# Loading the first keys by heads on two queues, and a finer list of operations, in a gated delta rule with a softplus block on one core

## The chip, the core and the metric

The program runs on one core of a Trainium2 chip. A core has five engines that run their own instruction streams in order and meet at semaphores: TensorE (PE, matmuls; PEld is its weight load), VectorE (DVE), ScalarE (ACT), GpSimd (POOL) and SyncE (SP). Transfers between device memory (HBM) and the on-chip memory (SBUF) run on 16 DMA engines and are issued by SP, ACT or POOL. Matmul results land in PSUM, here eight banks.

The metric is the device time of one execution in microseconds (us). A profile is one execution taken by the hardware profiler; its span goes from the first to the last instruction.

## The reference

Inputs are q, k, v and g of shape (4 batches, 8 heads, 768 steps, 48 features), beta of (4, 8, 768), and two weights: w_in (384, 2048) and w_out (2048, 384). All are float32.

```python
k_n = k / (np.linalg.norm(k, axis=-1, keepdims=True) + 1e-06)
state = zeros(B, H, D, D)
for t in range(S):
    readout = einsum('bhd,bhde->bhe', q[:, :, t], state)
    y[:, :, t] = g[:, :, t] * readout
    v_old = einsum('bhde,bhd->bhe', state, k_n[:, :, t])
    state = state + beta[:, :, t] * einsum('bhd,bhe->bhde', k_n[:, :, t], v[:, :, t] - v_old)
x = y.transpose(0, 2, 1, 3).reshape(B * S, H * D)
h = x @ w_in
out = (maximum(h, 0) + log1p(exp(-abs(h)))) @ w_out
```

The first part is a recurrence over 768 steps in 32 independent pairs of batch and head; the second is a dense block, two matmuls with a softplus between them.

## The kernel before

**Chunks.** The 768 steps are cut into 12 chunks of 64. Inside a chunk the recurrence becomes matrix algebra: the Gram matrix of the chunk's keys, a triangular system whose inverse is needed, and products with the state that the chunk before left. Two batches lie on the two halves of the 128 partitions (e = 0 and 1), two more side by side (p = 0 and 1), and each tile holds eight heads.

**The front of a chunk** (functions `norms` and `front`): the keys are squared (`ksq`, line 402) and summed per head (`red`, line 413), a square root and 1e-6 give the norms (`sqrt`, `eps`). The raw keys of chunks 0 and 1 are cast to 16 bits (`cast`; later chunks are scaled first, `kmul`), transposed by PE (`trs`, line 526), evicted from PSUM (`kev`), and the Gram matmuls follow (`gramk` for keys by keys, `gramq` for keys by queries, line 598). The key Gram is evicted with its sign turned (`kkc`, tile kk), the query Gram is masked (`mask`, tile mt). Chunks 0 and 1 do this in two halves of four heads.

**The inverse** (`inverse`) works on groups of chunks: 0, then 1, then pairs (2, 3), (4, 5) up to (10, 11); a group is named after its first chunk. The Gram is brought into lanes by 32 by 32 transposes on DVE (`ln`, line 656), picked (`pick`), and multiplied by beta (`prep`, line 697). `lbeta` prepares beta for the unscaled keys of chunks 0 and 1; it needs the selection matmuls `bsel` (line 287), which move beta from the partition of a head to lanes. Then come 15 steps j = 0 to 14 of a forward substitution: step 0 is one operation (line 709), every other a product into tmp (line 717) and an addition into tt (line 724), 29 operations in one serial string. They stand on DVE or POOL. `ca`, `cb` and `st` put the result back into matrix form (lines 738 and 779), and three rounds of PE matmuls (`xmm`, `tmm`, `zmm`) with evictions between them give the inverse of the whole chunk.

**The chain** (`chain`) is what carries the state from chunk to chunk: `ks` (state by keys, line 914), `w` (line 953), `umm`, `u1`, `zu`, `u2`, then `smm` and `s` (the new state, line 1010) and `qs`, `ymm` and `y` (the output times g, line 1036). `ytr` or a DMA transpose turns y into the columns of the dense block (tile xt).

**The dense block** (`dense`): `g1` multiplies by w_in into tile h (line 1088), `soft` is the softplus on ACT (line 1100), `g2` multiplies by w_out (line 1115), `o` evicts to tile osb, and `store` writes 64 rows at a time (line 1139).

**Order.** Nothing is scheduled by the hardware beyond the engines' own queues. Every piece of work is an item with a list of engines that may run it. The text `_ORDER` at the end of the file names each item once with its engine (D DVE, A ACT, G POOL, P PE, S SP); `Program.emit` walks through it and issues the items' instructions, so that the order on each engine is the order in that text. Tiles are taken from rings when an item first uses them and go back after the last use. An item that holds several instructions issues them together. Before the list the kernel issues a fixed head: the first beta load on ACT (line 184), the constants, and the identity.

Loads are items of SP (`load`, lines 326, 337 and 345). In this version chunk 0's keys are two loads, one for each half of the partitions:

```python
nc.scalar.dma_start(out=beta_n[:, : C * N_RAW], in_=beta_bt[:, : C * N_RAW])
```

```python
ENG[en].dma_start(
    out=b.ap[64 * e : 64 * e + 64].rearrange("t p h d -> t (p h) d"),
    in_=x[lo : lo + 2, :, ts].rearrange("p h t d -> t (p h) d"),
)
```

The list also holds filler matmuls (`fill`, line 1149), whose results nobody reads; of 96 that exist, `_ORDER` names 15.

## Time and profile before

| what | value |
|---|---|
| median of 3 timed runs | 295.17 us |
| the three runs | 381.88, 295.17, 240.01 us |
| the profiled execution | 239.09 us |
| its span, first to last instruction | 237.3 us |
| mean granted TensorE clock over the span | 0.984 |
| instructions | 11021 |
| HBM read and written | 25.26 and 4.72 MB |

The largest groups of instructions by busy time:

| group | instructions | busy us |
|---|---|---|
| g1, PE line 1088 | 384 | 74.0 |
| g2, PE line 1115 into tile o | 352 | 66.1 |
| softplus, ACT line 1100 | 96 | 56.5 |
| step products, POOL line 717 | 78 | 29.6 |
| step additions, POOL line 724 | 78 | 29.0 |
| powers for the norms, POOL line 427 | 8 | 23.5 |
| masks, DVE line 580 | 48 | 18.6 |

Rows of a timeline give the start in us from the beginning of the span, the length in us, the engine, the line, the operation, output and input tiles (buffer numbers left out), and in brackets how long the engine was idle before and what ended that. Consecutive instructions on one engine overlap slightly in these rows, since a row ends when the result is confirmed. A name such as SPq or ACTq is an engine's queue issuing a transfer. "issue" is time in which the engine waited for nothing that the profile shows. The chain of waits is followed back from the last instruction, step by step, to whatever released it.

### The profile page before, as it was taken

What the parts mean: (1) busy time and instruction counts of PE and PEld (TensorE: products, weight loads), DVE (VectorE), ACT (ScalarE), POOL (GpSimd) and SP (SyncE); (2) the same over time, 40 slices, a digit from 0 to 9 for tenths busy, and PEclk for the clock granted to TensorE, in tenths of its full rate; (3) what the DMA queues carried; (4) which work ended last, traced back from release to release, by engine and by line L of the source; (5) the groups of instructions that cost most, each with busy time, mean ns of one, the idle gap of its engine ahead of it and who ended that gap; (6) DMA issues with size and microseconds to landing.
All of it is one profiled execution on the core that took longest, in us unless ns stands there. A gap on an engine that the chain in (4) does not pass through costs nothing.

```text
span 237.3 us, 11021 instructions
## 1 busy us (share of the span) xinstructions
PE 206.0 (87%) x4787; PEld 130.4 (55%) x4787; DVE 162.8 (69%) x371; ACT 155.8 (66%) x332; POOL 115.3 (49%) x223
## 2 busy tenths in 40 slices
PE   4837865977987999989599999889999999999992
PEld 3723543754665665556355556455555555667761
DVE  7898994989978899995689768966648043521000
ACT  4999893955886789957189886348663766035520
POOL 5248989576767888988864763104721000000000
PEclk9999995999999999999999999999999999999999
DMA  6999999999899188789399676888635301242222
GB/s 117 179 196 171 194 205 210 185 146 188 151 181 149 37 150 153 204 134 151 86 162 154 119 143 77 130 174 155 116 89 115 69 7 33 64 92 50 53 50 66
DMA packets 101136, 30.30 MB, mean 128 GB/s; under 512 B 91808, under 2 KB 101056, under 8 KB 101088
## 3 DMA queue, kind: packets, MB, share of 16 engines
q1 hardware_dynamic: 96128, 24.96, 61.6%
q0 software_dynamic: 3712, 3.15, 9.3%
q10 hardware_dynamic: 1248, 1.49, 2.6%
q8 instruction: 37, 0.61, 1.1%
q14 instruction: 11, 0.09, 0.2%
HBM read 25.26 MB, written 4.72 MB: 126 GB/s over the span
## 4 chain that ended last, share of the span: by engine, by line
PE 63%; DVE 9%; issue 6%; ACT 6%; POOL 6%; DMA 5%; SPq 3%; DVEq 0%; ACTq 0%; POOLq 0%
PE h L1088 22%; PE o L1115 20%; PE d L598 3%; PE d L914 3%; PE d L1115 2%; SPq L345 2%; POOL tt L724 2%; DMA kqt<-kn 2%; POOL tmp L717 2%; PE d L1022 2%; DMA f<-in_k_dram 2%; ACT kk L222 2%; DMA f<-in_g_dram 2%; PE d L980 1%; DVE mt L580 1%
## 5 line engine op out<-in xcount | busy, mean ns | idle before, releaser
L1088 PE MATMUL h<-xt,w_in 128*128 128x512 f16 (+1 forms) x384 | 74.0, 330 | 0.3 <-DVE xt L224 0.2
L1100 ACT ACTIVATE ga<-h 128x512 f16<-128x512 f32 x96 | 56.5, 601 | 26.1 <-PE h L1088 21.2
L1115 PE MATMUL o<-w_out,ga 128*128 128x384 f16 x352 | 66.1, 327 | 0.0
L1115 PEld LDWEIGHTS <-ga 128*128 128x128 f16 x384 | 35.1, 98 | 22.3
L1088 PEld LDWEIGHTS <-w_in 128*128 128x128 f16 x384 | 35.1, 99 | 20.9 <-issue 0.7
L717 POOL TENSOR_TENSOR tmp<-nn,tt 128x56 f32<-128x56 f32 (+13 forms) x78 | 29.6, 379 | 19.9 <-DVE tt L724 12.1
L724 POOL TENSOR_TENSOR tt<-tt,tmp 128x56 f32<-128x56 f32 (+13 forms) x78 | 29.0, 372 | 6.1
L222 ACT ACTIVATE osb<-o 128x384 f32<-128x384 f32 x17 | 8.4, 492 | 25.1 <-PE o L1115 20.8
L427 POOL TENSOR_TENSOR nv<-nv,half_c 128x16 f32<-128x16 f32 x8 | 23.5, 2937 | 2.0 <-DVE nv L413 1.8
L580 DVE TENSOR_TENSOR mt<-d,mask 128x256 f16<-128x256 f32 x48 | 18.6, 410 | 4.8 <-ACT kk L222 2.2
L598 PE MATMUL d<-kqt 48*64 48x128 f16 (+1 forms) x448 | 11.4, 228 | 8.1 <-ACT kqt L222 4.6
L224 DVE CAST u<-d 128x384 f16<-128x384 f32 x21 | 11.4, 552 | 10.1 <-PE d L967 5.5
L1036 DVE TENSOR_TENSOR yg<-d,f 128x384 f16<-128x384 f32 x24 | 12.5, 546 | 8.4 <-ACT ga L1100 4.5
L222 ACT ACTIVATE u<-d 128x384 f16<-128x384 f32 x27 | 12.8, 494 | 6.0 <-PE d L980 3.2
L598 PEld LDWEIGHTS <-kqt 48*64 48x64 f16 x448 | 8.1, 118 | 14.8 <-issue 8.6
L222 ACT ACTIVATE kqt<-d 128x512 f16<-128x512 f16 (+1 forms) x23 | 14.1, 636 | 1.8 <-DVE w L953 0.8
L222 ACT ACTIVATE kk<-d 128x256 f16<-128x256 f32 x33 | 11.8, 385 | 4.9 <-PE d L598 3.1
L1010 DVE TENSOR_TENSOR s<-s,d 128x384 f16<-128x384 f16 x20 | 10.3, 542 | 5.8 <-PE d L996 5.4
L953 DVE TENSOR_TENSOR w<-f,d 128x384 f16<-128x384 f32 x22 | 11.5, 547 | 2.8 <-PE d L914 1.6
L413 DVE TENSOR_REDUCE nv<-f 128x16 f32<-128x768 f32 x12 | 11.2, 942 | 0.5 <-ACT f L402 0.5
L914 PEld LDWEIGHTS <-kqt 48*64 48x64 f16 x704 | 7.8, 108 | 6.2 <-issue 6.2
L914 PE MATMUL d<-s,kqt 48*64 48x48 f16 x704 | 9.7, 188 | 0.8 <-DVE qn L224 0.5
(134 smaller groups left out, 334.4 us busy)
## 6 DMA issues: line engine op xcount, KB each, us to landing
f<-in_k_dram SPq DMA_DIRECT2D x24, 192.0 KB, 7.5
f<-in_q_dram SPq DMA_DIRECT2D x24, 192.0 KB, 4.9
f<-in_v_dram SPq DMA_DIRECT2D x24, 192.0 KB, 4.7
out_dram<-osb SPq DMA_DIRECT2D x33, 96.0 KB, 3.4
f<-in_g_dram SPq DMA_DIRECT2D x24, 96.0 KB, 3.4
f<-in_g_dram SPq DMA_DIRECT2D x12, 192.0 KB, 5.6
w_in<-in_moe_w_in_dram POOLq DMA_DIRECT2D x4, 384.0 KB, 7.6
w_out<-in_moe_w_out_dram POOLq DMA_DIRECT2D x4, 384.0 KB, 8.9
```

What stands on the lines that cost most here:

```text
L222: nc.scalar.activation(o, x, AF.Copy, scale=float(sign))
L427: nc.gpsimd.tensor_tensor(nvs(), nvs(), half_c[:, :NU], ALU.pow)
L580: nc.vector.tensor_tensor(mt[c][p].ap[:, NP * g : NP * g + NP], bank(gb, p, n), mask[:, None, :].broadcast_to([P, NP, C]), ALU.mult)
L598: nc.tensor.matmul(o, kq(c, r, NP * g + i, FEAT[p], 0, C), x)
L717: ENG[en].tensor_tensor(t, nn.ap[:, :nb, j : j + 1, j + 1 :].broadcast_to([P, nb, w, n]), tt.ap[:, :nb, :w, j : j + 1].broadcast_to([P, nb ...
L724: ENG[en].tensor_tensor(rows, rows, t, ALU.add)
L914: nc.tensor.matmul(where(r, p)[:, h], kq(c, r, h, FEAT[p], off, off + C), s0[r].ap[FEAT[p], h], **start(h),)
L953: lambda en, p=p: nc.vector.tensor_tensor(w1[p].ap, vf.ap[:, p], hd(wp[p].ap), ALU.subtract),
L1036: lambda en, a=a: nc.vector.tensor_tensor(yg.ap[:, a], hd(yp[a].ap), gf.ap[:, a], ALU.mult),
L1088: nc.tensor.matmul(hp.ap[:, n * b : n * b + n], w_in[:, j, f * P : (f + 1) * P], xt.ap[:, j, t0 : t0 + n], start=(j == 0), stop=(j == 2),)
L1100: lambda en, hp=hp, o=gb: nc.scalar.activation(o.ap, hp.ap, AF.Softplus),
L1115: nc.tensor.matmul(op.ap[:, :DM], b.ap[:, col + c0 : col + c0 + 128], w_out[:, f, :], start=(f == 0), stop=(f == NF - 1),)
```

## The change

It has four parts.

1. **Chunk 0's keys.** A new function `first_keys` loads four heads of one half of the partitions, as two DMAs (one for each p). ACT issues both halves for e = 1 at the very head of its stream, ahead of the first beta load; the two items `k0.0` and `k0.1` on SP issue those for e = 0. A cast of four heads depends on its own item alone. The second beta load (`bload`) goes from SP to ACT in the order.
2. **Single operations as items.** A step's product and addition are two items, so that each may have another engine or other work between them. The same is done with `eps` and the reciprocal (`rcp`), the five operations of `lbeta`, the two lane transposes and the two picks of groups 0 and 1. The instructions are the same. `ca` and `cb` may also run on POOL.
3. **The last output.** Chunk 11's output at p = 0 was evicted in two copies of 192 columns, one on ACT and one on DVE; it is one copy of 384 columns. Item entries of `g2`, `o` and `store` are rewritten so that they could be made by columns, with one part each.
4. **Another `_ORDER`.** Of the 203 step operations DVE runs 89 instead of 43 and POOL 114 instead of 160. Step operations of group 0 change engine 8 times in place of 1, of group 4 8 times and of group 6 7 times in place of 0. Of the half-selecting copies `ca` and `cb` POOL runs 11 of 32 (before none). Two filler matmuls are named in place of 15. The loads stand in another order.

The new function and the core of the diff:

```diff
+    def first_keys(eng, t, e, half):
+        hs = slice(NP * half, NP * half + NP)
+        for p in range(2):
+            eng.dma_start(
+                out=t[64 * e : 64 * e + 64, p, hs],
+                in_=k[2 * e + p, hs, :C].rearrange("h t d -> t h d"),
+            )
+
+    for half in range(2):
+        first_keys(nc.scalar, r_f.tiles[0], 1, half)
     beta_bt = beta.rearrange("b h t -> (b h) t")
     nc.scalar.dma_start(out=beta_n[:, : C * N_RAW], in_=beta_bt[:, : C * N_RAW])
...
+        if name == "k" and c == 0:
+            for half in range(2):
+                part(f"{half}", lambda en, half=half: first_keys(ENG[en], b.ap, 0, half), 1025)
+            return
...
-                         deps=kl, bufs=[kf, kn[c]], size=768 // parts)
+                         deps=kl[h : h + 1] if c == 0 else kl,
+                         bufs=[kf, kn[c]], size=768 // parts)
...
-        for j in range(15):
-            prev = add("step", f"{tag}.{j}", en0, lambda en, j=j: step(en, j),
-                       deps=[prev], bufs=[nn, tt, tmp], size=nb * (15 - j) * (j + 1))
+        for j in range(15):
+            for k in range(2 if j else 1):
+                prev = add("step", f"{tag}.{j}.{k}", en0, lambda en, j=j, k=k: step(en, j, k),
+                           deps=[prev], bufs=[nn, tt, tmp] if k == 0 else [tt, tmp],
+                           size=nb * (15 - j) * (j + 1))
...
-                add("ca", f"{tag}.{x}", "DA",
+                add("ca", f"{tag}.{x}", "DAG",
...
-                parts = 2 if c == NC - 1 and p == 0 else 1
+                parts = 1
...
 _ORDER = """
-G0 D6 S22 D329 S23 D267 P213 D13 A234 A1 D16 S31 D14 P18 D19 D241 P242 G238 D235 S17 S33 P239
+S22 P18 A17 D15 D3 D8 D0 D19 S23 G11 G273 G238 D241 A234 P239 D6 D235 A236 S31 D237 D264 A240
...
```

Three places show what the order does. A row is an instruction with its line, operation, output and input tiles and size; numbers behind a tile's name are those of the built program.

The start of ACT's stream, before; L184 is the first beta load and L402 the squares of chunk 0's keys (tile f):

```order
L184 DMA w_out<-in_beta_dram 32x128
L186 ACT_TABLE_LOAD
L186 ACTIVATE dummy<-half_c 128x1
L222 ACTIVATE kk_101<-pat 128x16x32
L222 ACTIVATE td_129<-pat 128x16x32
L402 ACTIVATE f_78<-f_77 128x768
L222 ACTIVATE kk_101<-pat 128x16x32
L222 ACTIVATE kqt_104<-d_173 128x4x2x64
```

The same place after:

```order
L186 DMA f_77<-in_k_dram 64x4x48 x4
L194 DMA w_out<-in_beta_dram 32x128
L196 ACT_TABLE_LOAD
L196 ACTIVATE dummy<-half_c 128x1
L232 ACTIVATE kk_101<-pat 128x16x32
L232 ACTIVATE td_129<-pat 128x16x32
L307 DMA w_out<-in_beta_dram 32x640
L417 ACTIVATE f_78<-f_77 128x768
L434 ACTIVATE nv_95<-nv_95 128x32
L232 ACTIVATE kqt_104<-d_173 128x4x2x64
```

Four key loads stand ahead of the first beta load, the second beta load stands ahead of the squares, and the first eviction of keys (kqt) stands behind the square root (nv).

The start of PE's stream, before, one row of each run of equal work: beta selections (into d, from a part of w_out's tile), transposes of chunk 0's keys (kn) and its Gram matmuls (kqt):

```order
L1149 MATMUL h_177<-ident 128x512
L287 MATMUL d_172<-w_out 128x32 x4
L526 MATMUL d_173<-ident,kn_89 128x128
L526 MATMUL d_174<-ident,kn_89 128x128
L598 MATMUL d_175<-kqt_104 64x64
L598 MATMUL d_172<-kqt_104 64x64
L287 MATMUL d_174<-w_out 128x160 x4
```

The same after:

```order
L297 MATMUL d_172<-w_out 128x32 x4
L544 MATMUL d_173<-ident,kn_89 128x128
L297 MATMUL d_174<-w_out 128x160 x4
L544 MATMUL d_175<-ident,kn_89 128x128
L616 MATMUL d_176<-kqt_104 64x64
L616 MATMUL d_173<-kqt_104 64x64
```

The second beta selection has moved from behind chunk 0's Gram matmuls to between the two halves of its key transposes, and the filler matmul at the start is gone.

POOL's part of group 0's substitution, before; tt is the inverse under way, the row before the first L717 a cast of chunk 1's keys:

```order
L690 COPY tt_122<-bl_100 128x16
L224 CAST kn_90<-f_79 128x2x4x48
L717 TENSOR_TENSOR tmp_119<-nn_117,tt_122 128x63
L724 TENSOR_TENSOR tt_122<-tt_122,tmp_119 128x7x9
L717 TENSOR_TENSOR tmp_119<-nn_117,tt_122 128x64
```

After:

```order
L384 DMA w_in<-in_moe_w_in_dram 128x3x512
L724 COPY tt_121<-bl_100 128x16
L743 TENSOR_TENSOR tt_121<-nn_117,tt_121 128x15
L753 TENSOR_TENSOR tmp_119<-nn_117,tt_121 128x28
L760 TENSOR_TENSOR tt_121<-tt_121,tmp_119 128x2x14
L753 TENSOR_TENSOR tmp_119<-nn_117,tt_121 128x39
L760 TENSOR_TENSOR tt_121<-tt_121,tmp_119 128x3x13
L753 TENSOR_TENSOR tmp_119<-nn_117,tt_121 128x48
L234 COPY kk_102<-pat 128x16x32
L760 TENSOR_TENSOR tt_121<-tt_121,tmp_119 128x5x11
```

Before, DVE ran steps 0 to 5 and POOL the rest (from size 63). After, POOL begins with step 0, and from step 3 on DVE runs single operations between POOL's (the addition of size 4 by 12, for one, is missing here); a weight load (w_in) stands ahead of the substitution, where one stood inside it before.

More of the change, by code (lines that the diff above doesn't have):

```diff
@@ L684, in pick @@
             )
-        l1 = add("pick", tag, "D", pick, deps=[l1], bufs=[ln], size=256 if pair else 384)
+        for k in range(1 if pair else 2):
+            l1 = [add("pick", f"{tag}.{k}", "D", lambda en, k=k: pick(en, k), deps=l1, bufs=[ln],
+                      size=256 if pair or k == 0 else 128)]
+        l1 = l1[0]
         prev = add("clear", tag, "GD",
@@ L704, in prep, with step @@
             )
-        def step(en, j):
+        def step(en, j, k):
             n, w = 15 - j, j + 1
@@ L756, in inverse @@
                     cb.append(
-                        add("cb", f"{tag}.{x}{b}", "DA",
+                        add("cb", f"{tag}.{x}{b}", "DAG",
                             lambda en, x=x, b=b: masked(
@@ L771, in inverse @@
             cb.append(
-                add("cb", f"{tag}.{x}", "DA", both, deps=[prev], bufs=[tt, tw], size=512))
+                add("cb", f"{tag}.{x}", "DAG", both, deps=[prev], bufs=[tt, tw], size=512))
         def lanes_out(dst, src, blocks, step_):
@@ L1107, in dense @@
                 gi = 2 * (c % 2) + p
-                op = Buf(p_d) if c >= NC - 2 and p == 0 else Buf(p_o)
-                m2 = None
-                for f0 in range(0, NF, 4):
-                    def g2(en, f0=f0, op=op, c0=128 * gi - t0):
-                        for f in range(f0, f0 + 4):
-                            b, col = ga[f]
-                            nc.tensor.matmul(
-                                op.ap[:, :DM],
-                                b.ap[:, col + c0 : col + c0 + 128],
-                                w_out[:, f, :],
-                                start=(f == 0),
-                                stop=(f == NF - 1),
-                            )
-                    m2 = add("g2", f"{c}.{p}.{f0}", "P", g2,
-                             deps=[m2] + ga_it[f0 : f0 + 4] + [wl[1][f0 // 4]],
-                             bufs=[op] + [b for b, _ in ga[f0 : f0 + 4]], mm=4, mode="full")
@@ new lines, in dense, with g2, store @@
+                w = DM // parts
+                ob = Buf(r_o)
+                for x in range(parts):
+                    op = Buf(p_d) if c >= NC - 2 and p == 0 else Buf(p_o)
+                    cs_ = slice(w * x, w * x + w)
+                    sub = f"{c}.{p}" + (f".{x}" if parts > 1 else "")
+                    m2 = None
+                    for f0 in range(0, NF, 4):
+                        def g2(en, f0=f0, op=op, c0=128 * gi - t0, cs_=cs_):
+                            for f in range(f0, f0 + 4):
+                                b, col = ga[f]
+                                nc.tensor.matmul(
+                                    op.ap[:, cs_],
+                                    b.ap[:, col + c0 : col + c0 + 128],
+                                    w_out[:, f, cs_],
+                                    start=(f == 0),
+                                    stop=(f == NF - 1),
+                                )
+                        m2 = add("g2", f"{sub}.{f0}", "P", g2,
+                                 deps=[m2] + ga_it[f0 : f0 + 4] + [wl[1][f0 // 4]],
+                                 bufs=[op] + [b for b, _ in ga[f0 : f0 + 4]], mm=4, mode="full",
+                                 size=w)
+                    m3 = add("o", sub, "DA",
+                             lambda en, op=op, ob=ob, cs_=cs_: copy(
+                                 en, ob.ap[:, cs_], op.ap[:, cs_]),
+                             deps=[m2], bufs=[op, ob], size=w)
+                    for hf in range(2):
+                        def store(en, ob=ob, c=c, p=p, hf=hf, cs_=cs_):
+                            r0 = (2 * p + (hf ^ p)) * S + c * C
+                            ENG[en].dma_start(
+                                out=out[r0 : r0 + C, cs_], in_=ob.ap[64 * hf : 64 * hf + 64, cs_]
+                            )
+                        add("store", f"{sub}{hf}", "SA", store, deps=[m3], bufs=[ob])
```

245 lines of the change are left out of this document (126 added, 119 removed).

## The prediction

> **What bounds the kernel now.** I read the page first, then the busy time by stretches, then the timelines of single engines over the first 45 us. From the page: the span, the busy shares, the granted clock in 40 slices, and the chain of waits by engine.
>
> ```profile
> span 237.3 us, 11021 instructions
> PE 206.0 (87%) x4787; PEld 130.4 (55%) x4787; DVE 162.8 (69%) x371; ACT 155.8 (66%) x332; POOL 115.3 (49%) x223
> PEclk9999995999999999999999999999999999999999
> PE 63%; DVE 9%; issue 6%; ACT 6%; POOL 6%; DMA 5%; SPq 3%; DVEq 0%; ACTq 0%; POOLq 0%
> ```
>
> The profiled execution took 239.09 us: 237.3 of span and 1.8 around it. The sum below is made against it. It stands 0.4% under the shortest of the three timed runs (240.01), whose median is 295.17 only because the other two took 295.17 and 381.88; the trace shows nothing of where those two spent their time, so this forecast is for an execution like the profiled one. PE is the bound, but only as a share of the whole. Stretches show where it isn't (columns: stretch, length, then busy us of PE, PEld, DVE, ACT, POOL, granted clock, DMA share, GB/s):
>
> ```profile
> 40.00:50.00 10.00, 8.30 (x156) 6.35 (x156) 9.94 (x21) 7.05 (x15) 6.96 (x13) 0.89 1.36 189
> 50.00:60.00 10.00, 8.11 (x244) 5.22 (x246) 8.78 (x23) 6.22 (x13) 6.61 (x14) 1.00 1.13 152
> 60.00:70.00 10.00, 9.31 (x307) 6.90 (x306) 8.44 (x16) 8.83 (x23) 6.71 (x7) 1.00 0.96 171
> 70.00:80.00 10.00, 8.11 (x245) 5.71 (x244) 8.20 (x17) 6.13 (x15) 7.96 (x11) 1.00 0.82 131
> 100.00:110.00 10.00, 9.04 (x293) 5.48 (x291) 8.52 (x19) 6.89 (x16) 8.38 (x19) 1.00 0.93 157
> 110.00:120.00 10.00, 6.95 (x199) 4.68 (x197) 6.28 (x12) 3.46 (x8) 8.81 (x17) 1.00 0.60 101
> 150.00:160.00 10.00, 8.23 (x181) 4.73 (x179) 7.48 (x15) 4.07 (x11) 0.61 (x1) 1.00 0.80 137
> ```
>
> These seven rows are the ones between 40 and 160 us in which PE has holes: 1.70 + 1.89 + 0.69 + 1.89 + 0.96 + 3.05 + 1.77 = 12.0 us. Other cuts of the same span:
>
> ```profile
> 6.00:36.00 30.00, 21.01 (x466) 14.42 (x469) 27.86 (x80) 27.79 (x63) 20.04 (x50) 0.99 1.24 190
> 36.00:60.00 24.00, 18.15 (x422) 12.49 (x416) 19.73 (x46) 15.30 (x32) 17.19 (x32) 0.87 1.24 178
> 60.00:107.00 47.00, 43.44 (x1279) 28.04 (x1278) 42.22 (x80) 37.86 (x85) 38.40 (x58) 1.00 0.81 147
> 160.00:233.00 73.00, 72.68 (x1344) 45.01 (x1342) 27.96 (x60) 38.21 (x77) 9.49 (x24) 1.00 0.35 74
> ```
>
> So there are three stages. From 6 to 36 us DVE and ACT are both 93% busy and PE waits for them. To 160 us PE is nearly full with holes of 12 us. From 160 to 233 PE has no hole at all. What is lost or won must come from the start of dense work or from the 12 us.
>
> The front of the kernel, single instructions (start, length, engine, line):
>
> ```profile
> 0.81 0.39 ACTq L184 DMA_DIRECT2D w_out<-in_beta_dram  x1
> 1.62 4.10 DMA f<-in_k_dram
> 3.54 1.91 PE L287 MATMUL d<-w_out 32*128 32x32 f32 x8
> 5.81 0.84 ACT L402 ACTIVATE f<-f 128x768 f32<-128x768 f32 x1 [1.43 <-DMA f<-in_k_dram]
> 6.23 1.03 PE L526 MATMUL d<-ident,kn 128*128 128x128 f16 x8 [0.78 <-DVE kn L224]
> 7.56 0.41 DVE L224 COPY kqt<-d 128x512 f16<-128x512 f16 x1
> 7.71 0.74 PE L598 MATMUL d<-kqt 48*64 48x64 f16 x32 [0.44 <-ACT kqt L222]
> 8.38 2.49 PE L287 MATMUL d<-w_out 32*128 32x160 f32 x8
> 9.43 1.11 DVE L656 STREAM_TRANSPOSE ln<-kk 128x256 uint32<-128x256 uint32 x2
> 14.35 0.22 DVE L724 TENSOR_TENSOR tt<-tt,tmp 128x60 f32<-128x60 f32 x1
> 14.72 0.48 POOL L717 TENSOR_TENSOR tmp<-nn,tt 128x63 f32<-128x63 f32 x1 [4.56 <-DVE tt L724]
> 15.96 0.69 DVE L226 TENSOR_SCALAR kk<-d 128x256 f16<-128x256 f32 x2
> 20.76 1.00 POOL L369 DMA_DIRECT2D w_in<-in_moe_w_in_dram  x1
> 22.11 0.23 POOL L724 TENSOR_TENSOR tt<-tt,tmp 128x15 f32<-128x15 f32 x1
> 38.73 0.69 PE L1062 MATMUL d<-ident,yg 128*128 128x128 f16 x5 [2.11 <-issue]
> 40.07 3.14 PE L1088 MATMUL h<-xt,w_in 128*128 128x256 f16 x18 [0.22 <-DVE xt L224]
> ```
>
> Chunk 0's keys land at 5.72. Its inverse runs from 9.43 (lane transposes on DVE) to 22.34 (last step on POOL), 12.9 us. Dense work starts at 40.07.
>
> **Keys in halves, and what ACT and PE now do first.** The half loads are eight DMAs for two. ACT issues its four before the first beta load. A DMA on ACT's queue is priced by the stores (minimum/median/maximum in ns):
>
> ```profile
> L1139 ACTq DMA_DIRECT2D out_dram<-osb x15: 473/474/953, 145.7 to 233.9; - x15
> ```
>
> I take 0.5 us each. The beta load then goes out at 0.81 + 2.0 = 2.81 and is issued by 3.20 instead of 1.20. Before, it was there by 3.54, so it needs at most 2.34 after its issue; that puts the first beta selection at 5.54. PE's order ties the rest to it: selection 1 (1.91), half of the transposes (0.52), selection 2 (2.49, now *ahead* of the second half), the other half (0.52). That ends at 10.98. Then the DVE eviction (0.41), half of the Gram matmuls (0.37), two DVE evictions of kk (0.69) and some 0.3 for four handoffs: lane transposes at 12.75, not 9.43. Term: **+3.3 us**. Lower bound: if the beta load arrived as early as before the same string from 3.54 ends 2.0 earlier, +1.3; it can't be a gain, since those matmuls are in PE's own order. Upper: a landing of 4.10 as the key load's, +5.1. The middle is nearest to the only row for this very load. The second beta load also moves from SP to ACT, behind the table load and two copies; selection 1 and the first transposes cover it to 7.97, and a landing later than that would add to the upper bound.
>
> The Trainium skill, page "DMA: Bandwidth & Descriptors", section "Issuing engines are not separate DMA queues", says that transfers started by several engines run on the same 16 engines and that a second issuer saves issue time only. By that rule two queues bring the keys no more than some issue slots earlier, and the term stays; no run here shows it yet.
>
> **The inverse in single operations.** Chunk 0's 29 operations stood 11 on DVE and 18 on POOL; now 5 and 24, with 8 changes of engine for 1. Prices, from two rows of equal size:
>
> ```profile
> 52.36 0.29 DVE L717 TENSOR_TENSOR tmp<-nn,tt 128x128 f32<-128x128 f32 x1 [0.97 <-POOL tt L724]
> 84.63 0.43 POOL L717 TENSOR_TENSOR tmp<-nn,tt 128x128 f32<-128x128 f32 x1
> ```
>
> Six operations more on POOL: 6 x 0.14 = +0.8. A change of engine took 14.72 - 14.57 = 0.15, about 0.08 more than none: +0.6. The weight load of 1.00 that sat in the middle goes ahead: -1.0. DVE's operations now queue behind two reductions and a key scaling: +0.6. Together **+1.0** (-0.5 to +3, the latter if each DVE visit waits for a long instruction).
>
> From the inverse's end to dense work were 17.7 us, among them 2.11 us before 38.73 in which PE waited for nothing shown. That hole lies between two instructions of one loop, so another order need not meet it there: **-1.0** (-2.1 to +1). Dense work then starts at 43.4, **+3.3**.
>
> **The middle.** Over all groups 46 of 203 step operations go from POOL to DVE; the half-selecting copies of the inverse go partly from ACT to POOL. Groups 4 and 6 ran wholly on POOL; group 4:
>
> ```profile
> 78.31 0.24 POOL L709 TENSOR_TENSOR tt<-nn,tt 128x30 f32<-128x30 f32 x1
> 92.22 0.27 POOL L724 TENSOR_TENSOR tt<-tt,tmp 128x30 f32<-128x30 f32 x1
> ```
>
> That is 14.2 us. Now 11 of its 29 are DVE's: 11 x 0.14 less, 8 changes x 0.08 more, -0.9; group 6 (7 changes) the same. PE's order puts chunk 4's use of it ahead of about five dense blocks that stood before it. I take a part of the two gains, **-1.4**, of the 12.0 us of holes. Bounds: -8 (the holes that other engines made go) and +5 (next part).
>
> **Smaller terms.** Thirteen of 15 filler matmuls go; they stand in PE's waits and cost nothing by themselves. What ends them is cover for the clock, a rival below. The last output: two copies one after the other become one:
>
> ```profile
> 233.18 0.33 ACT L222 ACTIVATE osb<-d 128x192 f32<-128x192 f32 x1 [2.11 <-PE d L1115]
> 233.54 0.36 DVE L224 COPY osb<-d 128x192 f32<-128x192 f32 x1 [6.32 <-ACT osb L222]
> ```
>
> One of 384 columns, by interpolation about 0.5, ends at 233.7 for 233.9: **-0.2**. Square roots' additions and reciprocals, lane betas and picks only become separate entries with the same instructions: 0.
>
> **Sum:** 239.09 + 3.3 - 1.4 - 0.2 = **240.8 us**.
>
> **Rivals.** *DVE becomes the bound* (slower). Through group 6 DVE's step operations rise from 26 to 59: 33 x 0.27 = 8.9 us. Its idle time from 6 to 107 us is 2.1 + 4.3 + 4.8 = 11.2 us, and much of that is waits between PE and DVE. DVE's queue is in order, so every step behind an eviction of the chain waits for PE, and POOL's next step with it. If half of the 8.9 isn't covered, and the -1.4 doesn't come: 240.8 + 1.4 + 4.5 = 246.7. It decides from DVE 96% busy between 6 and 107 on. For it: DVE has 93% in the front; against it: ACT and POOL are relieved.
>
> *The middle absorbs all* (faster). The inverses run well ahead of the chain, and of the 12.0 us holes 8 go: 239.09 + 3.3 - 8.0 - 0.2 = 234.2. Against it: a part of the holes is PE's own issue, which no order of the others removes.
>
> *PE goes cold.* The fillers were not idle ballast: two of them took
>
> ```profile
> 21.32 1.04 PE L1149 MATMUL h<-ident 128*128 128x512 f16 x2
> 32.04 0.61 PE L1149 MATMUL h<-ident 128*128 128x512 f16 x2
> ```
>
> so PE worked at about half speed to 22 us and faster later, whatever the page's clock says there; the clock row shows one dip, at 36 to 42 us. Without fillers the front stays slow: five transposes of 1.03 for 0.61 (+2.1), and some 0.3 more in the first dense block, 243.2. The Trainium skill, page "TensorE: Matmul & The Clock Gate", section "Why this matters for your kernels", asks for no idle gaps over about 3 us on PE; these durations and the dip agree with it, and it speaks against the removal.
>
> *The keys do come early and matter*: casts and squares start before 5.8, PE's order doesn't bind, the +3.3 becomes -1.0 (a quarter of the 4.10, since half the keys are a half of the packets and selection 1 covers the rest): 236.5. Against it: the beta rows above.
>
> **How the numbers follow.** Chances: forecast 0.42, DVE bound 0.28, absorbed 0.14, cold 0.11, early keys 0.05. Two per cent, about what a measurement of this kernel can tell from no change, are 234.3 and 243.9. Slower is the DVE case and the forecast's own upper tail: 0.32. Faster is most of the absorbed case and a tail of the early keys: 0.13. The rest, 0.55, is within. The forecast's own range is 238 to 243.5. The whole range goes from the absorbed case, 234, to a little above the DVE case, 248.
>
> **What would show it.** First lane transposes of chunk 0 near 12.8 (right) or before 9.5 (early keys); selection 2 ahead of the second transposes and PE waiting for the beta load; the chunk 0 inverse 13 to 15 us long; first dense block at 42 to 45; PE holes between 40 and 160 us near 11 (forecast), under 5 (absorbed), over 15 with DVE above 96% (DVE bound); transposes of 1.03 us after 24 us (cold). I am wrong altogether if dense work starts by 40 us or PE has holes after 160.

## The result and the profile after

The changed kernel took 252.98 us (median of 4 runs, 251.34 to 253.88). The ratio to the kernel before is 1.047, with a 95% interval from 1.031 to 1.062: slower. Against medians of 240 to 242 us for the kernel before in the runs below, that is some 11 us, and it lies above the predicted range of 234 to 248. Medians here and below are over all runs of a kernel, while a ratio leaves out the slow ones, those over 1.5% above the kernel's fastest. The profiled execution took 253.72 us, 252.0 of it span.

The page of the changed kernel: span, busy shares, granted clock in 40 slices, chain of waits by engine.

```profile
span 252.0 us, 11036 instructions
PE 210.4 (83%) x4774; PEld 135.0 (54%) x4774; DVE 175.5 (70%) x412; ACT 149.0 (59%) x317; POOL 117.0 (46%) x197
PEclk9999999979979997999999999999999999999999
PE 68%; DVE 12%; ACT 6%; issue 5%; DMA 3%; POOL 3%; ACTq 1%; SPq 0%; DVEq 0%; POOLq 0%
```

PE's share fell from 87 to 83%. DVE has 12.7 us more work and ACT 6.8 us less. The front of the changed kernel in single rows (start, length, engine, line), from the issue of the keys to the first dense block:

```profile
0.79 3.04 ACTq L186 DMA_DIRECT2D f<-in_k_dram  x4
3.87 0.62 ACTq L194 DMA_DIRECT2D w_out<-in_beta_dram  x1
7.03 1.88 PE L297 MATMUL d<-w_out 32*128 32x32 f32 x8 [7.03 <-DMA w_out<-in_beta_dram]
9.38 2.50 PE L297 MATMUL d<-w_out 32*128 32x160 f32 x8
10.84 1.50 DVE L449 TENSOR_SCALAR nv<-nv 128x32 f32<-128x32 f32 x1 [0.29 <-ACT nv L434]
10.84 1.47 POOL L419 TENSOR_TENSOR f<-f 128x768 f32<-128x768 f32 x1
11.81 0.61 PE L544 MATMUL d<-ident,kn 128*128 128x128 f16 x4
14.82 0.62 DVE L681 STREAM_TRANSPOSE ln<-kk 128x256 uint32<-128x256 uint32 x1
28.65 0.42 POOL L760 TENSOR_TENSOR tt<-tt,tmp 128x15 f32<-128x15 f32 x1
32.26 0.23 PE L862 MATMUL d<-dn,kk 64*64 64x32 f16 x2 [1.46 <-DVE tt L760]
44.11 0.63 PE L1060 MATMUL d<-u,mt 64*64 64x48 f16 x32 [0.17 <-DVE u L234]
47.77 2.29 PE L1126 MATMUL h<-xt,w_in 128*128 128x256 f16 x12
```

The four key transfers occupy ACT's queue until 3.83, so the beta load goes out at 3.87, and PE's first instruction is selection 1 at 7.03; in the kernel before it stands at 3.54, behind a filler. Lane transposes start at 14.82 for 9.43, the inverse ends at 29.07 for 22.34, and dense work starts at 47.77 for 40.07. So 7.7 us are lost before the first dense block. Chunk 0's x product (row at 32.26) and y product (44.11) are the ends of its chain; in the kernel before they stand at

```profile
25.62 0.43 PE L824 MATMUL d<-dn,kk 64*64 64x32 f16 x32
33.78 0.44 PE L1022 MATMUL d<-u,mt 64*64 64x48 f16 x32
```

From x to y took 8.16 us and now takes 11.85; from y to dense work took 6.29 and now takes 3.66. The stages from here to the end (columns as in the prediction), the first row of the kernel before, the others of the changed kernel:

```profile
40.07:100.07 60.00, 53.88 (x1494) 36.30 (x1494) 54.61 (x109) 46.79 (x102) 46.12 (x72) 0.98 0.95 154
47.77:107.77 60.00, 47.85 (x1281) 33.69 (x1278) 49.89 (x109) 40.55 (x90) 41.28 (x55) 0.91 0.86 131
107.77:252.00 144.23, 138.67 (x3022) 82.54 (x3022) 86.48 (x193) 79.86 (x168) 44.15 (x70) 1.00 0.50 93
```

Dense start to end is 204.2 us, for 197.2 before: another 7.0 us, in an execution whose granted clock was 0.91 over 60 us. PE was busy 186.5 us of that stage, for 180.8 before, with the same work; its holes are 17.7 us, for 16.4.

### The profile page after: what moved, and what is told of

Read it like the earlier page. It is cut to its first block, busy times and chain, and to the rows that moved or that the text cites. A ratio compares the mean times of both kernels' runs of the same rounds, so it can differ in the third digit from the quotient of the medians.

```text
span 252.0 us, 11036 instructions
## 1 busy us (share of the span) xinstructions
PE 210.4 (83%) x4774; PEld 135.0 (54%) x4774; DVE 175.5 (70%) x412; ACT 149.0 (59%) x317; POOL 117.0 (46%) x197
## 4 chain that ended last, share of the span: by engine, by line
PE 68%; DVE 12%; ACT 6%; issue 5%; DMA 3%; POOL 3%; ACTq 1%; SPq 0%; DVEq 0%; POOLq 0%
PE h L1126 24%; PE o L1159 23%; PE d L952 3%; PE d L616 3%; PE d L1159 2%; DMA f<-in_v_dram 2%; DVE mt L598 2%; PE d L1060 2%; POOL tt L760 2%; PE d L862 2%; PE d L1018 1%; PE d L1034 1%; ACT ga L1138 1%; PE d L898 1%; PE d L915 1%
## 5 line engine op out<-in xcount | busy, mean ns | idle before, releaser
L1126 PE MATMUL h<-xt,w_in 128*128 128x512 f16 (+1 forms) x384 | 76.3, 336 | 1.8 <-issue 1.4
L760 POOL TENSOR_TENSOR tt<-tt,tmp 128x126 f32<-128x126 f32 (+15 forms) x59 | 23.1, 391 | 17.5 <-DVE tmp L753 12.5
L753 POOL TENSOR_TENSOR tmp<-nn,tt 128x126 f32<-128x126 f32 (+14 forms) x51 | 16.9, 332 | 17.4 <-DVE tt L760 13.5
L616 PE MATMUL d<-kqt 48*64 48x128 f16 (+1 forms) x448 | 14.0, 243 | 6.8 <-DVE mt L598 2.5
L232 ACT ACTIVATE kk<-d 128x256 f16<-128x256 f32 x36 | 12.7, 385 | 11.0 <-DVE mt L598 8.5
L234 DVE COPY osb<-o 128x384 f32<-128x384 f32 x5 | 2.8, 556 | 20.6 <-PE o L1159 20.6
L616 PEld LDWEIGHTS <-kqt 48*64 48x64 f16 x448 | 9.9, 127 | 12.5 <-issue 8.8
L753 DVE TENSOR_TENSOR tmp<-nn,tt 128x78 f32<-128x78 f32 (+13 forms) x47 | 11.7, 250 | 5.1 <-POOL tt L760 3.3
L478 PE MATMUL d<-ident,qn 128*128 128x128 f16 x80 | 7.9, 262 | 8.4 <-ACT qn L232 4.9
L952 PE MATMUL d<-s,kqt 48*64 48x48 f16 x704 | 10.6, 188 | 3.4 <-issue 2.9
L877 ACT ACTIVATE xs<-d,mk 128x128 f16<-128x128 f32 x32 | 9.6, 370 | 6.1 <-PE d L862 5.9
```

Of the source, the lines that this page charges most:

```text
L232: nc.scalar.activation(o, x, AF.Copy, scale=float(sign))
L234: ENG[en].tensor_copy(o, x)
L616: nc.tensor.matmul(o, kq(c, r, NP * g + i, FEAT[p], 0, C), x)
L753: ENG[en].tensor_tensor(t, nn.ap[:, :nb, j : j + 1, j + 1 :].broadcast_to([P, nb, w, n]), tt.ap[:, :nb, :w, j : j + 1].broadcast_to([P, nb ...
L760: ENG[en].tensor_tensor(rows, rows, t, ALU.add)
L952: nc.tensor.matmul(where(r, p)[:, h], kq(c, r, h, FEAT[p], off, off + C), s0[r].ap[FEAT[p], h], **start(h),)
```

## The experiments

Eighteen kernels were run (the number 12 is not used), each timed beside the kernel before on its chip. The ratio is to the kernel before, with its 95% interval; the last four columns are start times in us in the profiled execution.

| run | median us | ratio | lane transposes | x | y | dense |
|---|---|---|---|---|---|---|
| kernel before | 240.4 to 242.4 | 1 | 9.43 | 25.62 | 33.78 | 40.07 |
| changed kernel | 252.98 | 1.047 (1.031 to 1.062) | 14.82 | 32.26 | 44.11 | 47.77 |
| e1 beta first | 248.03 | 1.033 (1.022 to 1.044) | 11.58 | 29.50 | 41.35 | 45.89 |
| e2 fillers back | 253.20 | 1.045 (1.028 to 1.062) | 14.70 | 32.14 | 43.98 | 47.77 |
| e3 both | 250.94 | 1.047 (1.038 to 1.057) | 11.39 | 29.32 | 41.17 | 45.98 |
| e4 before, no fillers | 240.22 | 0.996 (0.982 to 1.010) | 9.47 | 25.37 | 34.66 | 38.69 |
| e5 keys whole | 247.50 | 1.035 (0.999 to 1.071) | 10.71 | 28.21 | 40.64 | 44.78 |
| e6 = e1, table load late | 250.84 | 1.044 (1.024 to 1.064) | 11.36 | 29.29 | 41.16 | 46.97 |
| e7 = e1, old step engines | 262.69 | 1.100 (1.089 to 1.111) | 11.49 | 31.00 | 43.33 | 48.17 |
| e8 before, with part 1 | 247.90 | 1.031 (0.997 to 1.066) | 14.98 | 31.34 | 39.35 | 42.97 |
| e9 = e5, w on VectorE | 248.15 | 1.035 (1.025 to 1.044) | 10.76 | 28.69 | 40.43 | 45.61 |
| e10 = e9, chunk 0 ahead | 249.86 | 1.044 (1.035 to 1.053) | 10.85 | 28.36 | 39.71 | 45.49 |
| e11 before, w split | 242.59 | 1.010 (1.001 to 1.020) | 9.43 | 25.80 | 36.01 | 40.04 |
| e13 = e9, steps to POOL | 249.09 | 1.024 (1.015 to 1.032) | 11.01 | 28.53 | 39.47 | 45.36 |
| e14 = e9, chain first | 248.34 | 1.026 (1.018 to 1.034) | 10.77 | 28.27 | 39.08 | 45.16 |
| e15 = e13 and e14 | 247.74 | 1.027 (1.020 to 1.033) | 10.74 | 28.26 | 39.14 | 46.31 |
| e16 = e9, old engines, no steps | 252.96 | 1.055 (1.046 to 1.064) | 11.60 | 33.67 | 46.01 | 49.29 |
| e17 before, new engines, no steps | 248.96 | 1.035 (1.028 to 1.042) | 10.25 | 32.07 | 45.22 | 49.50 |
| e18 new code, old order | 240.00 | 0.998 (0.993 to 1.003) | 9.56 | 25.93 | 33.91 | 38.79 |
| e19 before, keys in halves | 242.42 | 1.004 (0.998 to 1.009) | 10.03 | 26.26 | 34.42 | 38.81 |

**e1, beta first.** The front as I read it was the first suspect. In the table of order a letter is the engine and the number the item; 17 is the second beta load, 20 selection 2, which moves behind item 255, the second Gram product.

```diff
-    for half in range(2):
-        first_keys(nc.scalar, r_f.tiles[0], 1, half)
     beta_bt = beta.rearrange("b h t -> (b h) t")
     nc.scalar.dma_start(out=beta_n[:, : C * N_RAW], in_=beta_bt[:, : C * N_RAW])
+    for half in range(2):
+        first_keys(nc.scalar, r_f.tiles[0], 1, half)
...
-S22 P18 A17
+S22 P18
...
+S23 S17
...
-P20
 P242
...
 P255
+P20
```

> The changed kernel, but the first beta load is issued ahead of the keys on the scalar queue, the second one goes back to SP behind chunk 0's keys, and selection 2 stands behind the Gram products of chunk 0 in PE's order. Theory A (the front decides: beta is issued at 3.87 us behind four key transfers, and selection 2 sits between the halves): chunk 0's lane transposes move from 14.8 us to 9.5-11, and all behind them with it, so 4 to 5 us less than the changed kernel, 247 to 249 us. Rival B (the front's delay is taken up by waits before dense work, and the loss is made between 29 and 110 us): the lane transposes move as much, but dense work starts less than 1.5 us earlier than 47.8 us, 251 to 252.5 us.

Lane transposes start at 11.58, 3.2 us earlier, and the time falls by 4.9 us in the medians. Dense work starts only 1.9 earlier; the rest of the gain stands behind it, in an execution whose clock was 1.00 where the changed kernel's was 0.91. Theory A holds for the time; the lane transposes came out 0.6 us later than it said, and not all behind them moved with them.

**e2, fillers back; e3, both; e4, the kernel before without fillers.** The code of the fillers stands in both kernels; only the table names more of them or fewer. e2 puts thirteen ahead of the transposes of q0, q2, k3, q2 again, of chunk 0's x product and of one Gram product; e4 takes all fifteen out.

```diff
+P138 P139 P140
 P245
...
+P141 P142
 P415
...
+P143 P144
 P438
...
+P145 P146 P147
 P419
...
+P148 P149
 P315
...
+P150
 P440
```

> The changed kernel with 13 filler matmuls (128x512) put back into PE's waits between 15 and 41 us: three ahead of each of two groups of transposes, two ahead of each of three groups, one ahead of a Gram product. Theory C (PE cold without fillers): transposes after 24 us take 0.61 us for 1.03, Gram products 0.42 for 0.79, the first dense block of 12 matmuls 1.5 us for 2.29; dense work starts 2 to 4 us earlier than 47.8 and the time is 3 to 6 us less than the changed kernel, 247.5 to 250.5. Rival B (cold matmuls lie in waits that other engines set): the durations fall but the time stays within 1 us, 252 to 254.

> Both edits of the two runs before together. A and C both right and additive: 7 to 11 us less than the changed kernel, 242 to 246, so the rest to the kernel before is 2 to 6 us of strings of steps and order. If only A holds 247 to 249, if only C holds 247.5 to 250.5; if neither, about 252.

> The kernel before without its 15 filler matmuls, nothing else. Theory C (PE cold): 3 to 6 us slower than the kernel before, transposes between 26 and 49 us and Gram products between 24 and 36 us at their cold durations (1.03, 0.79). Rival (the fillers only fill): within 0.7 us of the kernel before.

Theory C fell by e4. Without fillers the kernel before runs its transposes cold, and the time is the same within the interval (0.996, 0.982 to 1.010). From its timeline, two rows whose like took 0.61 us with fillers:

```profile
26.15 1.04 PE L526 MATMUL d<-ident,kn 128*128 128x128 f16 x8
29.22 1.06 PE L461 MATMUL d<-ident,qn 128*128 128x128 f16 x8
```

e2 says less, since its fillers made PE fast only for a moment: one group of transposes took 0.62 us for 1.03, and the next ones were as slow as before. Two rows of e2, then one of the changed kernel:

```profile
25.47 0.62 PE L544 MATMUL d<-ident,kn 128*128 128x128 f16 x8 [0.33 <-DVE kn L527]
33.30 1.04 PE L544 MATMUL d<-ident,kn 128*128 128x128 f16 x8
```

```profile
33.42 1.03 PE L544 MATMUL d<-ident,kn 128*128 128x128 f16 x8
```

A stage of e2, then two stages of the changed kernel (the granted clock is the third number from the end):

```profile
30.00:50.00 20.00, 14.83 (x364) 10.28 (x365) 18.36 (x44) 14.82 (x33) 16.26 (x30) 0.50 1.26 199
```

```profile
20.00:30.00 10.00, 4.91 (x40) 3.93 (x40) 8.35 (x27) 4.33 (x9) 7.62 (x20) 1.00 1.25 178
30.00:50.00 20.00, 13.40 (x365) 10.13 (x365) 18.37 (x45) 14.96 (x33) 16.26 (x30) 1.00 1.25 202
```

The column shows 0.50 for e2 and 1.00 for the changed kernel, where the transposes above take the same time: a 1.00 in it does not say that PE runs at full speed. DVE, ACT and POOL do the same work in the same time in both. e3, with both edits, is 2.9 us above e1.

**e5, keys whole.** The first part undone altogether, on top of e1's places for beta and selection 2.

```diff
...
-        if name == "k" and c == 0:
-            for half in range(2):
-                part(f"{half}", lambda en, half=half: first_keys(ENG[en], b.ap, 0, half), 1025)
-            return
...
-                         deps=kl[h : h + 1] if c == 0 else kl,
+                         deps=kl,
```

> The changed kernel with its first part undone altogether: chunk 0's keys in two whole loads on SP, beta first on the scalar queue, the second beta load on SP, selection 2 behind the Gram products. Beyond the run with beta ahead of the keys (248.0 us) the scalar engine no longer issues four key transfers of 0.62 to 0.76 us. Theory A' (those issues delay its squares and copies): lane transposes of chunk 0 at 9.4 to 10.5 us for 11.58, time 246 to 247. Rival (the rest of the delay is the order of the setup instructions): lane transposes stay at 11 to 12 and the time at 247.5 to 249.

0.9 us at the lane transposes, half a microsecond in the median: the four issues on ACT cost little once beta is ahead of them. The interval of the ratio is wide and touches 1. Neither side of the expectation was met squarely; the rest of the delay is still there.

**e8 and e19, the first part in the kernel before.** e8 has the keys, both beta loads and selection 2 (item 20, ahead of the second transposes) as the change has them. e19 has the halves alone, the half that is cast first ahead, beta ahead of both, the second beta load on SP. The core of e8's edit:

```diff
...
+    for half in range(2):
+        first_keys(nc.scalar, r_f.tiles[0], 1, half)
     beta_bt = beta.rearrange("b h t -> (b h) t")
     nc.scalar.dma_start(out=beta_n[:, : C * N_RAW], in_=beta_bt[:, : C * N_RAW])
...
+A17
...
-S17
...
 S33
+P20
...
-P20
...
```

> The kernel before with the change's first part alone: chunk 0's keys in halves by heads on the scalar queue and SP, beta behind them on the scalar queue, the second beta load on the scalar queue, selection 2 ahead of the second group of transposes. Theory A: lane transposes of chunk 0 at 13 to 15 us for 9.43, time 4 to 6 us above the kernel before, 246 to 248. Rival (the kernel before has cover for it): less than 2 us above.

> The kernel before with chunk 0's keys in halves by heads on the scalar queue and SP, the half that is cast first ahead, but the first beta load ahead of the keys on the scalar queue, and the second one on SP as before. Theory A'' (the loss of the first part is beta's place and selection 2's, the halves as such cost little): lane transposes of chunk 0 at 9 to 10.5 us, time within 2 us of the kernel before, 240 to 243.5. Rival (issuing four key transfers on the scalar engine costs by itself): lane transposes at 11 us or more, 243.5 to 246.

The lane transposes of e8 and of e19:

```profile
14.98 1.11 DVE L672 STREAM_TRANSPOSE ln<-kk 128x256 uint32<-128x256 uint32 x2
```

```profile
10.03 1.12 DVE L672 STREAM_TRANSPOSE ln<-kk 128x256 uint32<-128x256 uint32 x2
```

So the first part's cost is beta's place behind four issues, with selection 2 between the halves: +5.6 us at the lane transposes and about +7 in the median (its ratio's interval, 0.997 to 1.066, just touches no change), while the halves by themselves cost 0.4%, at most 0.9. This is e1's result from the other side. How much is beta's and how much selection 2's was not tried.

**e6, table load late.** The chain of waits of e1 shows the activation table load (1.28 us) ahead of chunk 0's first u copy. Item 920 goes behind 928.

```diff
-A920
 A924
...
 A928
+A920
```

> The run with beta ahead of the keys, and in addition the activation table load (1.28 + 0.20 us, ahead of the first u copy of chunk 0 on the scalar engine) moved behind chunk 0's second u copy, where the kernel before had it. Theory D (it stands on chunk 0's chain): x product to y product of chunk 0 takes 1.0 to 1.6 us less than 11.85, dense work starts as much earlier than 45.89, time 246.3 to 247.2. Rival (PE waits for the mask products of VectorE there anyway): 247.5 to 248.5.

x to y took 11.87 us, as before: theory D fell. The time, 250.84, is no better either.

**e7, the steps on their old engines.** Every step operation and every half-selecting copy gets the letter of the kernel before, 106 in all; for example

```diff
-D561
+G561
...
-G306
+A306
```

> The run with beta ahead of the keys, and in addition every step operation of the inverses, and every half-selecting copy behind them, on the engine that it had before (106 operations change their engine; the order stays). Theory E (strings that change between VectorE and POOL make the inverses late): chunk 0's inverse takes 12.5 to 13.5 us for 14.74, group 2's less than 14, and the time is 244 to 246. Rival (the strings are not what dense work waits for, or POOL alone is as slow): 247.5 to 249.5.

14.7 us slower than e1. Chunk 0's inverse took 16.1 us (11.49 to 27.61) for 14.74. Theory E had the wrong sign for this order: in the changed kernel's order these 106 choices of engine are worth a lot.

**e9, e11, the w products.** In e5 a w product took 1.88 us on VectorE, beside one on POOL. e9 puts both on VectorE, e11 splits them in the kernel before.

```diff
-G921
 D922
+D921
```

```diff
-D809
+G809
```

> The run with the keys whole, and in addition both first products w of chunk 0 on VectorE, as before the change (one moves from POOL, ahead of nothing else). Theory F (VectorE and POOL slow each other: the w product took 1.88 us on VectorE beside POOL's 0.83, 0.55 and 0.66 when both stood on VectorE): both take 0.55 to 0.7, the mask product behind them comes 0.7 us earlier, dense work starts 0.5 to 1.0 us earlier than 44.78, time 246 to 247 beside 247.5. Rival: the same work in one queue takes as long, 247.3 or more.

> The kernel before with one of chunk 0's two w products on POOL instead of VectorE, nothing else. Theory F: the one left on VectorE takes 0.9 to 1.9 us for 0.55 and POOL's 0.8 to 1.3; time 0 to 1.5 us above the kernel before. Rival (independent engines): VectorE's 0.55 stays, POOL's about 0.8 us, and the time stays within 0.3 us.

The rows of e5, of e9 (both in one row) and of e11:

```profile
32.31 1.88 DVE L978 TENSOR_TENSOR w<-f,nv 128x384 f16<-128x384 f32 x1
32.93 0.83 POOL L978 TENSOR_TENSOR w<-f,nv 128x384 f16<-128x384 f32 x1
```

```profile
32.71 1.37 DVE L978 TENSOR_TENSOR w<-f,nv 128x384 f16<-128x384 f32 x2
```

```profile
29.90 0.55 DVE L947 TENSOR_TENSOR w<-f,nv 128x384 f16<-128x384 f32 x1
31.87 0.83 POOL L947 TENSOR_TENSOR w<-f,nv 128x384 f16<-128x384 f32 x1
```

Where the two overlap, VectorE's is long; in e11 they did not overlap, and it kept its 0.55. e11 therefore doesn't test theory F. In it POOL comes to its product only at 31.87, and x to y takes 10.21 us, yet dense work starts at 40.04, as in the kernel before: two more microseconds between x and y were taken up behind y, and where e11's 1.0% comes from is not shown. In e9 the two together are shorter than one in e5, but dense work starts no earlier.

**e10, e13, e14, e15, chunk 0's chain put ahead.** All four stand on e9. e10 moves the table load behind the u copies and the u copies (925, 927) ahead of a reduction (513); e13 puts nine steps on POOL; e14 takes the Gram products of chunks 2 and 3 with their masks (445, 440, 422 and theirs) behind the y product (932); e15 has e13 and e14.

```diff
 P923
+D925
...
 D259
+P926 D927 D513
...
 A928
+A920
```

```diff
-D369 D370 D373 D374 D377 D378 D379 D381 D382
+G369 G370 G373 G374 G377 G378 G379 G381 G382
```

```diff
+P258
 P318
...
-P445
...
-P440
...
-P422
 P932
+P445
...
+P440
...
+P422
```

> The run before, and chunk 0's chain put ahead in the queues: the activation table load behind its second u copy on the scalar engine, on VectorE its two u copies ahead of a reduction (0.94 us) and of two steps of the next inverse. Theory G (what is left of the loss is chunk 0's chain, x to y product 12.4 us for 8.2 in the kernel before, because its evictions stand behind masks, steps and the table load): x to y 9 to 10.5, dense work starts 2 to 3 us earlier than 44.78 and the time is 244 to 245.5. Rival H (the loss left is in the middle, in the order of the later chunks): dense work starts earlier but the end does not, 246.5 to 248.

> The run with keys whole and both w products on VectorE, and nine steps of chunk 1's inverse (1.6 to 1.12) moved from VectorE to POOL, where they stood between chunk 0's evictions and masks. Theory I (chunk 0's chain is held by these steps, because they wait for POOL in VectorE's queue): x to y product of chunk 0 falls from 11.7 to 9.5-10.5 us, dense work starts 1 to 2 us earlier than 45.6, time 246 to 247. Rival J (it is held by PE's own order, Gram products of chunks 2 and 3 that wait for masks): x to y stays within 0.7 us, the inverse of chunk 1 gets longer, time 248 or more.

> The run with keys whole and both w products on VectorE; the steps stay where they are, but chunk 0's last q Gram product comes ahead of its t product, the Gram products of chunks 2 and 3 with their masks behind chunk 0's y product, its evictions first, the table load behind them. Theory J: x to y product 8 to 9.5 us for 11.7, dense work starts 2 to 4 us earlier than 45.6, the time is 244.5 to 246.5 (group 2's inverse starts later and takes a part back). Rival I: x to y stays above 11.

> Both edits of the two runs before. If both hold part of the chain: x to y near the 8.2 us of the kernel before, dense work starts at 41 to 42.5 us, time 243 to 245.5. If the time stays at 247 or more although dense work starts by 42.5, the loss that is left comes from the later chunks (rival H).

x to y came down from 11.74 (e9) to 11.35, 10.94, 10.81 and 10.88, and dense work started at 45.49, 45.36, 45.16 and 46.31 for 45.61. Theories G and I fall, and J in its size: nothing in this chain gives back more than 1 us, and not more than 0.45 us of that reaches dense work. The four medians lie between 247.7 and 249.9; the ratios of e13 to e15, 1.024 to 1.027 beside e9's 1.035, leave room for one per cent. (The profiled execution of e14 took 351 us at a granted clock of 0.56 from 146 us on; only its first 50 us, at 1.00, are read here.)

**e16, e17, the other operations' engines.** Up to dense work the changed kernel has more on VectorE and POOL than the kernel before. The stretch of the kernel before, of the changed kernel, and of e16:

```profile
0.00:40.07 40.07, 25.20 (x485) 17.23 (x486) 33.68 (x106) 32.63 (x71) 26.82 (x67) 0.94 1.16 182
```

```profile
0.00:47.77 47.77, 23.88 (x487) 18.80 (x487) 39.09 (x112) 28.54 (x60) 31.56 (x74) 1.00 1.12 187
```

```profile
0.00:49.29 49.29, 23.92 (x487) 18.94 (x487) 33.89 (x111) 32.67 (x71) 26.18 (x66) 1.00 1.12 186
```

e16 gives 43 of these operations in e9 the letter that they had before, e17 gives 41 in the kernel before the new one. For example, in e16 and in e17:

```diff
-G306
+A306
```

```diff
-A304
+G304
```

> The run with keys whole and both w products on VectorE, and 43 operations ahead of the first dense block (pattern fills, squares, casts, evictions, key scalings, half-selecting copies; no step of an inverse) on the engine that they had before the change; the order stays. Theory K (until dense work starts the changed kernel has 5.4 us more on VectorE and 4.7 us more on POOL, 4.1 us less on ACT, and VectorE is busy 15.4 of the 16.9 us of chunk 0's chain): VectorE and POOL have 3 to 6 us less before dense work, which starts 2 to 4 us earlier than 45.6; time 244 to 246. Rival L (the place in the queues is what counts, engines alone do not help in this order): dense start within 1 us or later, 247.5 or more.

> The kernel before with 41 of the same operations on the engines that they have in the changed kernel (the two half-selecting copies that went to POOL stay on ACT); its own order, keys and fillers. Theory K: dense work starts 2 to 4 us later than 40.07, time 2 to 5 us above the kernel before. Rival L: it may be anything above, since each order suits its own engines, 3 to 10 us above. If the engines do not matter, within 1 us.

e16 has the old kernel's work on VectorE, ACT and POOL to within 0.7 us, and dense work starts 3.7 us *later* than in e9. Theory K, that VectorE and POOL are overloaded, falls. e17 is 3.5% slower. This is what rival L said: an order suits the engines that it was made for, and these halves of one kernel in the other lose. Why was not traced.

**e18, the new code in the old order.** The last question was whether the finer list of operations costs anything by itself. e18 has the changed kernel's single operations and its one copy of the last output, keys whole, and the table of the kernel before, in which an entry that is now several stands as these, one behind the other, on its old engine. Beside the changed kernel's table, chunk 4's second step is an example:

```diff
-D561
...
-D562
+G561 G562
```

> The changed kernel's single operations and its one copy of the last output, in the order and on the engines of the kernel before, both operations of a step one behind the other, fillers included, keys whole on SP. Theory M (what is left beside the keys is the new table of order and engines as a whole, and the division into single operations costs nothing by itself): within 1.5 us of the kernel before, 240 to 243 us, chunk 0's x to y product 8 to 8.5 us, dense work from 39 to 41. Rival N (more, smaller entries cost waits of their own): 245 or more, steps further apart than the 0.07 to 0.08 us of the kernel before.

240.00 us, ratio 0.998 (0.993 to 1.003). x and y product and dense start of e18:

```profile
25.93 0.61 PE L855 MATMUL d<-dn,kk 64*64 64x32 f16 x32
33.91 0.44 PE L1053 MATMUL d<-u,mt 64*64 64x48 f16 x32
38.79 3.25 PE L1119 MATMUL h<-xt,w_in 128*128 128x256 f16 x18 [0.22 <-DVE xt L232]
```

x to y is 7.98 us. Theory M holds: the division, the separate entries and the one copy cost nothing. With e19 (halves) and e4 (fillers) every part but two is priced at nothing, to within the intervals, which reach 1% at most. The two are beta's place with selection 2 (4.9 us by e1's median, 3 by the ratios) and the new table of order and engines as a whole: e5 and e9 lack the first and still stand 3.5% above, 6 to 8 us (e9's interval is 1.025 to 1.044). In their profiles this loss lies ahead of dense work: e9 reaches it at 45.61, e18 at 38.79, and from there to the end e9 takes 198.3 us and e18 199.4. The two prices add up to 11 us within their intervals. No version beat the kernel before by more than its interval.

## Why the prediction was wrong

**The front, +3.3 (+1.3 to +5.1).** The mechanism was right, step by step: selection 1 waits for beta, selection 2 stands ahead of the second transposes. The size wasn't: +5.4. Two terms were mis-sized. Four issues on ACT took 3.04 us, not 2.0, since I had priced loads by stores; with a slower landing selection 1 came at 7.03 for 5.54. From there to the lane transposes I had 7.21 us and the trace has 7.79: the addition on VectorE took 1.50 us beside POOL's square, which I had at nothing, and the copy of the second half's keys stood behind it in the queue.

**The inverse, +1.0.** It took 14.25 us for 12.91: +1.3, well within the bounds.

**From the inverse's end to dense work, -1.0 (-2.1 to +1).** The first of two failed steps. It was 18.70 us for 17.73, so +1.0. The hole of 2.11 us did not come back, as I had hoped, and from y to dense work took 2.6 us less; but chunk 0's chain from x to y took 3.7 us more. I had compared the hole and not the chain: the new order of three engines between x and y stood in the table and no term of the sum was made of it. Six runs (e6, e9, e10, e13 to e15) tried to say which entry does it. Each moved about 1 us at most, so it is shown that the whole table does it (e18) and not shown how. e11, where x to y grew by 2.05 us and dense work started no later, says besides that this length is not all that dense work waits for.

**The middle, -1.4 (-8 to +5).** The second failed step, and by size the largest miss, 8.4 us. The trace shows +7.0. The sum took PE's own work as fixed and the holes as what could be won; instead the holes came out 1.3 us larger and PE's busy time 5.7 us longer. The clock of 0.91 is three stretches of about 3.4 us at 0.50, between 52.5 and 56.5, 69.5 and 73.5, 97 and 101 us. In the first of them twelve products took 2.65 us, behind it 1.47:

```profile
53.86 2.65 PE L1126 MATMUL h<-xt,w_in 128*128 128x256 f16 x12
57.19 1.47 PE L1126 MATMUL h<-xt,w_in 128*128 128x256 f16 x12
```

At half speed each stretch can cost 1.7 us, the three 5.1 (an estimate). That they make the time is argued, not shown: unprofiled runs at a mean clock of 0.99 took 251.3 and 253.9 us, those at 0.98 252.2 and, profiled, 253.7. What is shown is that the gain isn't there: with the clock at 1.00, e1 takes 199.8 us from dense start to the end and e9 198.3, e18 with the old order 199.4. So the new strings win nothing behind dense start. Why the changed kernel loses there 4.4 us more than e1 stays open.

**Fillers and the last copy, 0 and -0.2.** Right, the first within e4's interval. From the last copy to the end took 4.1 us before and 4.0 after.

**The rivals.** The cold PE was right in its durations (1.03 us after 24 us, as listed) and, by e4, wrong in its price. The dip of the clock at 36 to 42 us, which it read as agreeing with the rule on idle gaps, does not tell a cold PE: e4 has a granted clock of 1.00 up to 38.69 us and runs its transposes cold. VectorE as the bound gave the nearest time, 246.7, but its sign isn't there: PE's holes between 40 and 160 us are indeed over 15, 15.9 us, but VectorE is busy 83.8 of the 101 us between 6 and 107, 83% and not 96, and e16 says no. The early keys brought nothing: in e19 the lane transposes are at 10.03. The Trainium skill's rule (page "DMA: Bandwidth & Descriptors", section "Issuing engines are not separate DMA queues"), cited in the prediction, agrees with that: two issuers saved no landing that counted. The time to issue, which the page calls usually small beside the transfer, was here 3.04 us for four loads, and the beta load stood behind them.

**The range.** Each term had its own upper end, and the range took only one rival's. All upper ends together, 5.1 + 3 + 1 + 5 on 239.09, less 0.2, are 253.0. That this is the measured time is luck: the four came out at 5.4, 1.3, 1.0 and 7.0.

## What to carry to other kernels

Issue the small load that the first matmul waits for ahead of the large ones on its queue, and price each issue by a load's row, not a store's. When a change brings a new order and new code at once, put the new code into the old order first: one run then says whether the code or the order is to be looked at. Make a term for every stretch whose order changes, not only for the hole that may go. A table of order and its choice of engines is one thing; moving half of it back, by position or by engine, lost more often than it won.

## What the runs showed of the hardware

VectorE and POOL hold each other up. Besides the addition (1.50 for 0.18 us) and the w product (1.88 for 0.55), in the changed kernel a step on POOL, whose neighbour of nearly that size took 0.30, took 0.94 beside a key scaling on VectorE:

```profile
24.11 0.30 POOL L760 TENSOR_TENSOR tt<-tt,tmp 128x60 f32<-128x60 f32 x1
24.74 0.94 POOL L760 TENSOR_TENSOR tt<-tt,tmp 128x55 f32<-128x55 f32 x1 [0.33 <-DVE tmp L753]
24.58 0.95 DVE L527 TENSOR_TENSOR kn<-f,nv 128x768 f16<-128x768 f32 x1
```

The Trainium skill, page "GPSIMD Engine Reference", section "8. Key points", says that GpSimd shares its SBUF interfaces with VectorE and meets contention from VectorE instructions with two SBUF inputs or in a two-port mode. The w product and the key scaling have two SBUF inputs, and their rows agree; the addition has one, and no run here shows which mode it ran in. Two of the long rows end where the neighbour ends: the addition at 12.34 us and POOL's square at 12.31, the step at 25.68 and the key scaling at 25.53.

Fillers are not a free way to keep PE fast. Thirteen matmuls between 15 and 41 us came with a granted clock of 0.50 from 30 to 50 us (e2, and e3 too), and a transpose that ran cold without them (1.03 us) ran at 1.04 with them, one earlier at 0.62. The Trainium skill, page "TensorE: Matmul & The Clock Gate", section "Why this matters for your kernels", asks for no idle gaps over about 3 us. The changed kernel has a gap of 3.83 us ahead of the cold transposes at 20.41 us, which fits; in e4 the longest gap between 11 and 29 us is 2.6 us, and the transposes are cold all the same. The time of e4 shows no gain, within 1.4%, from fast transposes where PE isn't what is waited for.

The granted clock has to be read beside durations. Eight 128x128 transposes took 1.03 us in the changed kernel at 25.59 us and 0.61 in the kernel before at 26.24, and the column shows 1.00 for both (20 to 30 us).
